# Dummy matmuls in two forced waits, a changed bias copy, and an output sum prepared ahead, in a fused transformer block

## The chip, the core and the metric

The kernel runs on one core of one Trainium2 chip. The core has a matrix engine (TensorE, PE in the profile, with its weight loads shown as PEld), a vector engine (VectorE, DVE), an engine for activation functions (ScalarE, ACT), a general one (GpSimd, POOL) and a sync engine (SP) that issues the DMAs here. Each engine runs its own list of instructions in order and waits on semaphores for the others. Matmuls write to PSUM, which has 8 banks of 512 float32 columns on 128 partitions. The metric is the device time of one execution, in microseconds.

## The reference

The input x is [1, 2048, 1024] in bf16; there are 32 heads of width 32, and the hidden width of the second half is 3584.

```python
h  = x + A(layernorm(x))
h2 = h + B(layernorm(h))

def A(x):                                   # attention, no mask
    q, k, v = split(x @ wqkv)               # 32 heads of 32
    p = softmax(q @ k.T * 32 ** -0.5)
    return (p @ v) @ wo

def B(x):                                   # feed-forward
    return gelu(x @ w1 + b1, tanh form) @ w2 + b2
```

## The kernel before

**A planner writes the order.** The Python code does not call the engines directly. `plan.task` appends an instruction to the list of its engine, works out which semaphores it must wait for, and adds its estimated `cost` to a clock for that engine (`plan.free`). `plan.ready` says when the inputs and the bank of a possible next step should be there. A loop (from line 1751) picks TensorE's next step by these planned times. The order is therefore fixed when the kernel is built, and a changed cost can change it.

**Stages.** First, all 2048 rows are normalized and transposed, and the first keys, queries and values are made (to about 52 us). Then comes the attention stage: 512 units, each for one group of 4 heads, 256 queries and 256 keys. One unit is a burst of 8 matmuls for scores (`qk`, line 1121, recorded at L1130) into 4 banks, then two exponentials on ScalarE over two banks each (L1139). The score banks are 0 to 5, as three pairs that rotate, so a burst can be issued as soon as the exponential that read the pair before has ended. The products with V and the row sums (`pv`, L1215) go to bank 6. For some units VectorE first adds the two halves of the exponentials (`fold`, L1164), which saves TensorE one of four steps. "Quad" below means four matmuls side by side on 32 output partitions each.

**Filling.** Between the bursts TensorE does "fill" work: first the remaining keys, queries and values, later the output projection and the whole feed-forward part (`ffn`, line 1463) of the query block before. Fill has only bank 7, so each result must be copied out by VectorE before the next fill starts. There are four query blocks of 512 rows; the fourth block's feed-forward part is the tail, after the last exponential (`tail`, line 1643).

**Forced waits.** Before a new group of heads starts in the first query block, its largest key norm must be known, because the exponential's bias is made from it. `until(mark, lax)` (line 1050) then runs pending `pv` steps and fill until the mark is there: a key projection, its copy to KT and its square on VectorE (lines 582, 583), the sums of squares (`sumsq`, line 628), a diagonal matrix (`spread`, line 643), a matmul with the ones matrix, a maximum (line 646) and the bias (`bias_of`, line 672).

**Feed-forward.** For each of 28 slices of 128 hidden columns, `evac` (line 1537) copies the bank to `gT`, adds b1 and halves (L1538). Per two slices a chain of four operations makes the gelu (L1550 to L1553; L1552 is a tanh on ScalarE). With y = x/2 the halved copy is used on both sides of the formula, so no factor is left at the end. `rows_out` (line 1429) multiplies by w2, adds b2 from the bank (L1448), adds the residual `hch` (L1451), and stores. `early_slices` makes 6 pairs of slices of the fourth block ahead of the tail (L1638).

**Tail.** Its gelu is one ScalarE instruction (L1678), and its output goes through `rows_out` as well: 8 calls, each for two row tiles and 256 output columns, with 56 matmuls into one bank. `load_b2` comes after the last weights in SP's list.

Of the kernel before, what the change touches and what calls it, by code (L numbers as in the profile page):

```python
# [235 lines left out]
def build_kernel(nc, A_x, A_wqkv, A_wo, B_w1, B_b1, B_w2, B_b2, out):  # L236
# [9 lines left out]
    SCALE = DH ** -0.5  # L246
    SAFE = 70.0
    EPS_BF = 1.0013580322265625e-05
    GC = 8.0 * 0.044715
    GB = 2.0 / GC  # L250
    GK = GC * math.sqrt(2.0 / math.pi)
    QF = 3.0
    KEEP = 7
# [796 lines left out]
    def until(mark, lax=False):  # L1050
        while mark not in marks:
            service(plan.free[E.PE])
            t = plan.free[E.PE]
            if lax and pending and fill_ready() > t + 60:
                e = sums[0] if sums and (due_sum() or plan.ready(E.PE, pv_reads(sums[0]), []) <= t + 150) else pending[0]
                if all(m_ in marks for m_ in v_marks(e)) and plan.ready(E.PE, pv_reads(e), [B_ps[OD]] if starts(e) else []) <= t + 150:
                    pv()
                    continue
            if not do_fill():
                raise RuntimeError(f"never made: {mark}")  # L1060

    biased = set()
    pending = deque()
# [365 lines left out]
    def rows_out(ci, q, t, w2_, gT, B_g, g_ch, ost, B_ost, hch, B_hch, b2s, coming=None):  # L1429
# [6 lines left out]
        for lo_fc, hi_fc, u in ((0, cut, 0), (0, cut, 1), (cut, FC, 0), (cut, FC, 1)):  # L1436
            lo = (t + u) * P
            for fc in range(lo_fc, hi_fc):
                if fc % 8 == 0 and coming:
                    coming.popleft()()  # L1440
                if fc % 2 == 0:
                    yield Need(B_g(fc) + B_g(fc + 1) + [B_w2_[fc // 2]], [B_ps[bank]] if u == 0 and fc == 0 else [],
                               [g_ch[fc + 1]] if fc + 1 in g_ch else [])
                wide(bank, u * 256, 256, gT[:, fc, lo:lo + P], w2[:, fc, :], fc == 0, fc == FC - 1,
                     B_g(fc) + [B_w2_[fc // 2]], [B_ps[bank]] if fc in (0, FC - 1) else [], fc == FC - 1, quad)
        o = (q * 2 + t // 2) % len(B_ost)
        b2_, B_b2_ = b2s
        dve(lambda v: v.tensor_tensor(ost[:, o, :, :], ps[:, bank, :].rearrange("p (u c) -> p u c", u=2),  # L1448
                                      b2_[:, q * 256:(q + 1) * 256].unsqueeze(1).to_broadcast([P, 2, 256]), ALU.add),
            reads=[B_ps[bank]] + B_b2_, writes=[B_ost[o]], cost=690)  # L1450
        add = (E.DVE, lambda v: v.tensor_tensor(ost[:, o, :, :], ost[:, o, :, :], hch[:, t:t + 2, q * 256:(q + 1) * 256], ALU.add),  # L1451
               [B_ost[o]] + [B_hch[2 * (t + u) + q // 2] for u in range(2)], [B_ost[o]], 430)
        r0 = CH[ci][0] + t * P

        def store():
            dma(out2[r0:r0 + 2 * P, q * 256:(q + 1) * 256].rearrange("(u p) c -> p u c", p=P), ost[:, o, :, :], 131072,
                reads=[B_ost[o]], lanes=lanes_o, is_out=True)
            if ci < NCH - 2 and q % 2:
                for u in range(2):
                    load_rows(r0 + 512 + u * P, t + u, q // 2)  # L1460
        stores.append(chain([add, ("call", store, [B_ost[o]], [], 0)]))

    def ffn(ci):
# [62 lines left out]
        for bk in range(FC // 2):  # L1526
            s = w1s[bk]
            for u in range(2):
                fc = bk * 2 + u
                if u == 1:  # L1530
                    load_w1(bk + len(B_w1_) - 1)
                if fc == FC // 2:
                    w2s = [load_w2(ci, 0, f["w2_off"])]
                if fc >= FC // 2:
                    w2s[0][2].popleft()()

                def evac(bank, fc=fc):
# [74 lines left out]
    def early_slices():  # L1612
        if early["stop"]:
            return
        tail_gelus()
        gT, B_gT = early["gT"]
        w1, B_w1_ = early["w1"]
        hn, B_hn = last["hn", 0]
        coming = early["coming"]
        while early["n"] < FC // 2 - AHEAD and not early["stop"]:  # L1620
            bk = early["n"]
            early["n"] += 1
            if bk:
# [12 lines left out]
            for u in range(2):  # L1636
                fc = 2 * bk + u
                dve(lambda v, fc=fc, u=u: v.tensor_scalar(gT[:, fc, 0:256], ps[:, bank, u * 256:u * 256 + 256], b1f[:, fc:fc + 1], None, ALU.add),  # L1638
                    reads=[B_ps[bank], Bf_b1f], writes=[B_gT[2 * fc]], cost=420)
        while coming:  # L1640
            coming.popleft()()

    def tail():
# [83 lines left out]
            load_more()  # L1727
        while rest:
            rest.popleft()()
        b2s = load_b2(LAST, v_off + 28672)  # L1730
        ost, B_ost = sb("ost_t", [P, 8, 2, 256], dt.bfloat16, nbufs(8), at=f["x3_off"])
        hch, B_hch = last["hch"]
        for q in range(4):
            for t in (0, 2):
                yield from rows_out(LAST, q, t, w2s[q], gT, lambda fc: [B_gT[2 * fc + t // 2]], {}, ost, B_ost, hch, B_hch, b2s)
            if q < 2:
                w2s.append(load_w2(LAST, q + 2, v_off + q * 14336, True))

# [12 lines left out]
    while u < NU or pending:  # L1751
# [199 lines left out]
```

## Time and profile before

| what | value |
|---|---|
| runs shown | 1149.47, 1150.96, 1151.28 us; median 1150.96 us |
| profiled execution, its own time | 1149.56 us |
| its span, first to last instruction | 1147.8 us |
| PE busy / ACT busy / DVE busy | 1086.5 / 1042.0 / 683.3 us |
| mean granted TensorE clock | 0.996 |
| exponentials L1139 | 1024 instructions, 952.0 us busy, mean 1145 ns of one |
| copies L1538 | 84 instructions, 63.0 us busy, mean 750 ns |

The times of instructions on one engine overlap (an exponential takes 1145 ns, but the next starts before it has ended), so busy time is not count times mean. "Idle before" is the time in which the engine stood still ahead of the instruction, with the instruction that ended it. The granted clock (PEclk) is 1.00 at full speed and 0.50 at half.

### The profile page before, as it was taken

What the parts mean: (1) busy time and instruction counts of PE and PEld (TensorE: products, weight loads), DVE (VectorE), ACT (ScalarE), POOL (GpSimd) and SP (SyncE); (2) the same over time, 40 slices, a digit from 0 to 9 for tenths busy, and PEclk for the clock granted to TensorE, in tenths of its full rate; (3) what the DMA queues carried; (4) which work ended last, traced back from release to release, by engine and by line L of the source; (5) the groups of instructions that cost most, each with busy time, mean ns of one, the idle gap of its engine ahead of it and who ended that gap; (6) DMA issues with size and microseconds to landing.
All of it is one profiled execution on the core that took longest, in us unless ns stands there. A gap on an engine that the chain in (4) does not pass through costs nothing.

```text
span 1147.8 us, 54608 instructions
## 1 busy us (share of the span) xinstructions
PE 1086.5 (95%) x25370; PEld 658.6 (57%) x25370; DVE 683.3 (60%) x1219; ACT 1042.0 (91%) x1158; POOL 21.2 (2%) x59
## 2 busy tenths in 40 slices
PE   6999999899998999999999999999999999999998
PEld 3646456464444445767444446675544476676887
DVE  8564565555666778545567787545678755556011
ACT  7798999899999999999999999999999999996410
POOL 2100000000000000000000000000000000000000
PEclk9999999999999999999999999999999999999999
DMA  9201000003341244342613343321223332426923
GB/s 264 58 21 40 15 9 3 21 4 103 67 85 58 76 117 115 92 122 60 135 30 95 90 126 99 96 82 31 77 77 109 107 110 72 83 81 187 246 79 87
DMA packets 197941, 98.43 MB, mean 86 GB/s; under 512 B 53328, under 2 KB 194640, under 8 KB 197712
## 3 DMA queue, kind: packets, MB, share of 16 engines
q1 hardware_dynamic: 197712, 94.93, 30.9%
q8 instruction: 198, 3.24, 1.2%
q14 instruction: 31, 0.25, 0.1%
HBM read 88.09 MB, written 4.19 MB: 80 GB/s over the span
## 4 chain that ended last, share of the span: by engine, by line
ACT 50%; PE 33%; issue 10%; DVE 6%; DMA 0%; POOL 0%; ACTq 0%; DVEq 0%; POOLq 0%
ACT PT L1139 47%; PE ps L529 13%; PE ps L524 8%; PE ps L1215 5%; PE ps L1130 4%; ACT tm L1552 3%; DVE lnst L481 1%; PE ps L803 1%; DVE Rg L1228 1%; DVE Rg L1226 1%; DVE QT L1230 1%; PE ps L858 1%; DVE rcp L1227 0%; DVE gT L1538 0%; DVE gT L1553 0%
## 5 line engine op out<-in xcount | busy, mean ns | idle before, releaser
L1139 ACT ACTIVATE PT<-ps 128x1024 bf16<-128x1024 f32 x1024 | 952.0, 1145 | 13.4 <-DVE biasm L681 9.7
L1164 DVE TENSOR_TENSOR FS<-PT 128x1024 bf16<-128x1024 bf16 x252 | 172.2, 688 | 146.7 <-ACT PT L1139 119.0
L1215 PE MATMUL ps<-PT,V 128*32 128x256 bf16 x4096 | 224.9, 274 | 11.6 <-ACT PT L1139 6.1
L1130 PE MATMUL ps<-QT,KT 32*128 32x256 bf16 x4096 | 203.9, 273 | 18.1 <-ACT PT L1139 14.5
L529 PE MATMUL ps<-hnT,w 128*32 128x512 bf16 x2688 | 172.6, 381 | 6.1 <-DVE gT L1538 4.5
L529 PE MATMUL ps<-w,gT 128*32 128x256 bf16 x5376 | 172.6, 273 | 0.7 <-issue 0.6
L1130 PEld LDWEIGHTS ps<-QT,KT 32*128 32x128 bf16 x4096 | 61.1, 92 | 168.0 <-ACT PT L1139 157.7
L529 PEld LDWEIGHTS ps<-w,gT 128*32 128x32 bf16 x5376 | 141.1, 97 | 10.5 <-issue 5.6
L1215 PEld LDWEIGHTS ps<-PT,V 128*32 128x32 bf16 x4096 | 106.0, 96 | 62.0 <-ACT PT L1139 16.2
L1215 PE MATMUL ps<-PT,ones 128*32 128x256 bf16 x2080 | 132.3, 274 | 0.0
L529 PEld LDWEIGHTS ps<-hnT,w 128*32 128x32 bf16 x2688 | 61.5, 96 | 75.5 <-issue 28.4
L1538 DVE TENSOR_SCALAR gT<-ps,b1f 128x512 bf16<-128x512 f32 x84 | 63.0, 750 | 46.0 <-PE ps L529 44.4
L1215 PE MATMUL ps<-FS,ones 128*32 128x256 bf16 x1008 | 72.4, 277 | 0.0
L1215 PEld LDWEIGHTS ps<-PT,ones 128*32 128x32 bf16 x2080 | 56.4, 97 | 10.1
L529 PE MATMUL ps<-xnTe,wk 128*32 128x512 bf16 x832 | 56.6, 395 | 4.3 <-DVE kmax L646 2.3
L1553 DVE SCALAR_TENSOR_TENSOR gT<-tm,gT 128x1024 bf16<-128x1024 bf16 x42 | 51.1, 1219 | 1.4 <-ACT tm L1552 1.0
L1551 DVE SCALAR_TENSOR_TENSOR tm<-tm,gT 128x1024 bf16<-128x1024 bf16 x42 | 51.3, 1222 | 0.9
L1552 ACT ACTIVATE tm<-tm 128x1024 bf16<-128x1024 bf16 x42 | 50.1, 1193 | 0.0
L524 PE MATMUL ps<-w,gT_t 128*128 128x256 bf16 x448 | 49.1, 273 | 0.0
L1448 DVE TENSOR_TENSOR ost_t<-ps,b 128x512 bf16<-128x512 f32 x8 | 5.5, 692 | 72.6 <-PE ps L524 72.6
L524 PEld LDWEIGHTS ps<-w,gT_t 128*128 128x128 bf16 x448 | 43.8, 98 | 5.1
L1678 ACT ACTIVATE gT_t<-ps,b1f 128x256 bf16<-128x256 f32 (+1 forms) x36 | 17.2, 518 | 28.5 <-PE ps L524 28.5
(140 smaller groups left out, 931.4 us busy)
## 6 DMA issues: line engine op xcount, KB each, us to landing
w<-in_B_w_dram SPq DMA_DIRECT2D x42, 512.0 KB, 3.8
w<-in_B_w_dram SPq DMA_DIRECT2D x168, 128.0 KB, 3.6
w_t<-in_B_w_dram SPq DMA_DIRECT2D x12, 512.0 KB, 6.7
xr<-in_A_x_dram SPq DMA_DIRECT2D x16, 256.0 KB, 6.9
wk<-in_A_wqkv_dram SPq DMA_DIRECT2D x16, 256.0 KB, 3.2
wq<-in_A_wqkv_dram SPq DMA_DIRECT2D x16, 256.0 KB, 4.7
w_e<-in_B_w_dram SPq DMA_DIRECT2D x32, 128.0 KB, 2.4
w<-in_B_w_dram SPq DMA_DIRECT2D x14, 256.0 KB, 5.5
```

The costliest lines, as they stand in the source:

```text
L481: steps.append((E.DVE, lambda v, c=c: v.bn_stats(lnst[:, s, i, c * 6:(c + 1) * 6], x_ap[:, c * 512:(c + 1) * 512]), [B_x], [B], 690))
L524: pe(lambda p: p.matmul(ps[:, bank, lo:lo + n], lhsT, rhs, start=start, stop=stop), reads=reads, writes=writes, inc=inc, cost=mm(n))
L529: pe(lambda p, r=r: p.matmul(ps[32 * r:32 * r + 32, bank, lo:lo + n], lhsT[:, 32 * r:32 * r + 32], rhs, start=start, stop=stop, tile_posit ...
L1130: pe(lambda p, k=k, kt=kt, r=r, b=b: p.matmul(ps[:, b, k * 256:(k + 1) * 256], KT[32 * r:32 * r + 32, g, kt * P:(kt + 1) * P], QT[32 * r:3 ...
L1139: act(lambda a, safe, i=i, b=b: a.activation(PT[:, o_, 2 * i:2 * i + 2, :], ps[:, b:b + 2, :], ACT.Exp, bias=0.0 if safe else biasm[:, g, ...
L1164: dve(lambda v: v.tensor_tensor(FS[:, f_, :, :], PT[:, o_, :, 0:256], PT[:, o_, :, 256:512], ALU.add), reads=B_PT[o_], writes=[B_FS[f_]], ...
L1215: pe(lambda p, d=d, r=r, lhsT=lhsT, rhs=rhs, n=n: p.matmul(ps[32 * r:32 * r + 32, OD, d * 256:(d + 1) * 256], lhsT, rhs, start=(start and ...
L1538: dve(lambda v: v.tensor_scalar(gT[:, fc, 0:w], ps[:, bank, 0:w], b1f[:, fc:fc + 1], 0.5, ALU.add, ALU.mult), reads=[B_ps[bank], Bf_b1f], ...
L1551: (E.DVE, lambda v: v.scalar_tensor_tensor(t_, t_, GB, x_, ALU.add, ALU.mult), [Bt] + Bx, [Bt], 1220),
L1552: (E.Activation, lambda a: a.activation(t_, t_, ACT.Tanh, scale=GK), [Bt], [Bt], 946),
L1553: (E.DVE, lambda v: v.scalar_tensor_tensor(x_, t_, 1.0, x_, ALU.add, ALU.mult), [Bt] + Bx, Bx, 1220)])
L1678: act(lambda a: a.activation(gT[:, fc, lo:lo + n], ps[:, bank, o:o + n], ACT.Gelu_apprx_tanh, bias=b1f[:, fc:fc + 1], scale=1.0), reads=[B ...
```

## The change

There are three parts.

1. A new function `awake(t)` is called with the planned time of TensorE's next useful step, in `until` where that is a forced wait, and in the main loop where ScalarE has nothing left by the plan. As long as more than 330 ns of planned waiting are left, it adds one quad that multiplies the ones matrix by itself (512 columns) into the first bank of the next score burst. That burst starts a new sum there, so nothing of it is kept.
2. The copy with b1 becomes a two-tensor addition, whose second operand is b1's column repeated over the slice, without the halving (84 copies in `ffn`, 12 in `early_slices`). The constants of the gelu change to match, and the factor 0.5 moves into the b2 addition of `rows_out`, which becomes a three-operand instruction. The planned cost of a copy goes from 714 to 690.
3. In the tail, residual and b2 are summed ahead into `hb` (4 additions on VectorE, float32, at `xl_off`, in memory that held output-projection weights whose use has ended). Each output bank is then read once, by one addition, instead of two additions, and stored at once, in the list's order. The last of the 8 output steps is split into its two row tiles, each with a bank, an addition of 256 columns and a store of 64 KB of its own.

```diff
-    GC = 8.0 * 0.044715
-    GB = 2.0 / GC
+    GC = 0.044715
+    GB = 1.0 / GC
...
+            if lax:
+                awake(fill_ready())
             if not do_fill():
                 raise RuntimeError(f"never made: {mark}")
+
+    def awake(t):
+        b = qk_banks(u)[0]
+        while t < INF and max(plan.free[E.PE], plan.ready(E.PE, [], [B_ps[b]])) + 330 < t:
+            for r in range(4):
+                pe(lambda p, r=r: p.matmul(ps[32 * r:32 * r + 32, b, :], ones_pp[:, 0:32], ones_pp[:].unsqueeze(1).to_broadcast([P, 4, P]),
+                                           start=True, stop=True, tile_position=(0, 32 * r), skip_group_check=True),
+                   reads=[B_ones], writes=[B_ps[b]] if r in (0, 3) else [], inc=r == 3, cost=mm(512) if r == 0 else 1, kind="C")
...
+        if ci == LAST:
+            hb, B_hb = b2s
+            if lone is not None:
+                r0, t, o = r0 + lone * P, t + lone, (o + lone) % len(B_ost)
+                dve(lambda v: v.tensor_tensor(ost[:, o, lone, :], ps[:, bank, lone * 256:lone * 256 + 256], hb[:, t, q * 256:(q + 1) * 256], ALU.add),
+                    reads=[B_ps[bank], B_hb[t]], writes=[B_ost[o]], cost=430)
+                dma(out2[r0:r0 + P, q * 256:(q + 1) * 256], ost[:, o, lone, :], 65536, reads=[B_ost[o]], lanes=lanes_o, is_out=True)
+                return
...
-        dve(lambda v: v.tensor_tensor(ost[:, o, :, :], ps[:, bank, :].rearrange("p (u c) -> p u c", u=2),
-                                      b2_[:, q * 256:(q + 1) * 256].unsqueeze(1).to_broadcast([P, 2, 256]), ALU.add),
+        dve(lambda v: v.scalar_tensor_tensor(ost[:, o, :, :], ps[:, bank, :].rearrange("p (u c) -> p u c", u=2), 0.5 if ci < LAST else 1.0,
+                                             b2_[:, q * 256:(q + 1) * 256].unsqueeze(1).to_broadcast([P, 2, 256]), ALU.mult, ALU.add),
...
-                    dve(lambda v: v.tensor_scalar(gT[:, fc, 0:w], ps[:, bank, 0:w], b1f[:, fc:fc + 1], 0.5, ALU.add, ALU.mult),
-                        reads=[B_ps[bank], Bf_b1f], writes=[B_gT[fc]], cost=100 + 1.2 * w)
+                    dve(lambda v: v.tensor_tensor(gT[:, fc, 0:w], ps[:, bank, 0:w], b1f[:, fc:fc + 1].to_broadcast([P, w]), ALU.add),
+                        reads=[B_ps[bank], Bf_b1f], writes=[B_gT[fc]], cost=690)
...
+        hb, B_hb = b2s = sb("hb", [P, 4, D], dt.float32, nbufs(4), at=xl_off)
+        for t4 in range(4):
+            dve(lambda v, t4=t4: v.tensor_tensor(hb[:, t4, :], hch[:, t4, :], b2_[:], ALU.add),
+                reads=B_hch[2 * t4:2 * t4 + 2] + B_b2_, writes=[B_hb[t4]], cost=1220)
         for q in range(4):
-            for t in (0, 2):
+            for t, lone in (((0, None), (2, None)) if q < 3 else ((0, None), (2, 0), (2, 1))):
...
             best = min(q_r, p_r if p_r + TURN + step <= due else INF, f_r if f_r + TURN + step <= due else INF)
+            if plan.free[E.Activation] <= t:
+                awake(best)
```

More of the change, by code (lines that the diff above doesn't have):

```diff
@@ L1427, in load_b2, with rows_out @@
         return b2_, B
-    def rows_out(ci, q, t, w2_, gT, B_g, g_ch, ost, B_ost, hch, B_hch, b2s, coming=None):
+    def rows_out(ci, q, t, w2_, gT, B_g, g_ch, ost, B_ost, hch, B_hch, b2s, coming=None, lone=None):
         w2, B_w2_, parts = w2_
@@ L1436, in rows_out @@
         for lo_fc, hi_fc, u in ((0, cut, 0), (0, cut, 1), (cut, FC, 0), (cut, FC, 1)):
+            if lone is not None and u != lone:
+                continue
             lo = (t + u) * P
@@ L1441, in rows_out @@
                 if fc % 2 == 0:
-                    yield Need(B_g(fc) + B_g(fc + 1) + [B_w2_[fc // 2]], [B_ps[bank]] if u == 0 and fc == 0 else [],
+                    yield Need(B_g(fc) + B_g(fc + 1) + [B_w2_[fc // 2]], [B_ps[bank]] if u == (lone or 0) and fc == 0 else [],
                                [g_ch[fc + 1]] if fc + 1 in g_ch else [])
@@ L1446, in rows_out @@
         o = (q * 2 + t // 2) % len(B_ost)
+        r0 = CH[ci][0] + t * P
+        if ci == LAST:
[6 more added lines that the diff above has]
+                return
+            dve(lambda v: v.tensor_tensor(ost[:, o, :, :], ps[:, bank, :].rearrange("p (u c) -> p u c", u=2), hb[:, t:t + 2, q * 256:(q + 1) * 256], ALU.add),
+                reads=[B_ps[bank]] + B_hb[t:t + 2], writes=[B_ost[o]], cost=690)
+            dma(out2[r0:r0 + 2 * P, q * 256:(q + 1) * 256].rearrange("(u p) c -> p u c", p=P), ost[:, o, :, :], 131072,
+                reads=[B_ost[o]], lanes=lanes_o, is_out=True)
+            return
         b2_, B_b2_ = b2s
-        dve(lambda v: v.tensor_tensor(ost[:, o, :, :], ps[:, bank, :].rearrange("p (u c) -> p u c", u=2),
-                                      b2_[:, q * 256:(q + 1) * 256].unsqueeze(1).to_broadcast([P, 2, 256]), ALU.add),
+        dve(lambda v: v.scalar_tensor_tensor(ost[:, o, :, :], ps[:, bank, :].rearrange("p (u c) -> p u c", u=2), 0.5 if ci < LAST else 1.0,
+                                             b2_[:, q * 256:(q + 1) * 256].unsqueeze(1).to_broadcast([P, 2, 256]), ALU.mult, ALU.add),
             reads=[B_ps[bank]] + B_b2_, writes=[B_ost[o]], cost=690)
@@ L1452, in rows_out @@
                [B_ost[o]] + [B_hch[2 * (t + u) + q // 2] for u in range(2)], [B_ost[o]], 430)
-        r0 = CH[ci][0] + t * P
         def store():
@@ L1637, in early_slices @@
                 fc = 2 * bk + u
-                dve(lambda v, fc=fc, u=u: v.tensor_scalar(gT[:, fc, 0:256], ps[:, bank, u * 256:u * 256 + 256], b1f[:, fc:fc + 1], None, ALU.add),
+                dve(lambda v, fc=fc, u=u: v.tensor_tensor(gT[:, fc, 0:256], ps[:, bank, u * 256:u * 256 + 256], b1f[:, fc:fc + 1].to_broadcast([P, 256]), ALU.add),
                     reads=[B_ps[bank], Bf_b1f], writes=[B_gT[2 * fc]], cost=420)
@@ L1729, in tail @@
             rest.popleft()()
-        b2s = load_b2(LAST, v_off + 28672)
+        b2_, B_b2_ = load_b2(LAST, v_off + 28672)
         ost, B_ost = sb("ost_t", [P, 8, 2, 256], dt.bfloat16, nbufs(8), at=f["x3_off"])
         hch, B_hch = last["hch"]
+        hb, B_hb = b2s = sb("hb", [P, 4, D], dt.float32, nbufs(4), at=xl_off)
+        for t4 in range(4):
+            dve(lambda v, t4=t4: v.tensor_tensor(hb[:, t4, :], hch[:, t4, :], b2_[:], ALU.add),
+                reads=B_hch[2 * t4:2 * t4 + 2] + B_b2_, writes=[B_hb[t4]], cost=1220)
         for q in range(4):
-            for t in (0, 2):
-                yield from rows_out(LAST, q, t, w2s[q], gT, lambda fc: [B_gT[2 * fc + t // 2]], {}, ost, B_ost, hch, B_hch, b2s)
+            for t, lone in (((0, None), (2, None)) if q < 3 else ((0, None), (2, 0), (2, 1))):
+                yield from rows_out(LAST, q, t, w2s[q], gT, lambda fc: [B_gT[2 * fc + t // 2]], {}, ost, B_ost, hch, B_hch, b2s, lone=lone)
             if q < 2:
```

## The prediction

> **What bounds the kernel now.** I read the page first (busy times and groups), then busy time by stretch, then the timeline where ScalarE stands still, then the timeline of the end.
>
> ```profile
> PE 1086.5 (95%) x25370; PEld 658.6 (57%) x25370; DVE 683.3 (60%) x1219; ACT 1042.0 (91%) x1158; POOL 21.2 (2%) x59
> ...
> L1139 ACT ACTIVATE PT<-ps 128x1024 bf16<-128x1024 f32 x1024 | 952.0, 1145 | 13.4 <-DVE biasm L681 9.7
> ```
>
> ScalarE's 91% hides two stages. From 52 us (first exponential) to 1046 us it almost never stops: 13.4 us of idle in front of 1024 exponentials, 9.7 of them in two waits for the bias. From there to the end TensorE is the bound. So the change can gain in three places only: those 13.4 us, the tail's matmuls, and what follows the last matmul. VectorE is at 60%, and shorter work on it gains nothing unless ScalarE waits for it.
>
> The two waits for the bias, from the timeline; each line has start, length, engine and operation, count, and idle before:
>
> ```profile
> 116.19 1.94 ACT L1139 ACTIVATE PT<-ps 128x1024 bf16<-128x1024 f32 x2 [4.84 <-DVE biasm L681]
> ...
> 119.34 1.94 ACT L1139 ACTIVATE PT<-ps 128x1024 bf16<-128x1024 f32 x2 [1.21 <-PE ps L1130]
> ...
> 210.80 1.94 ACT L1139 ACTIVATE PT<-ps 128x1024 bf16<-128x1024 f32 x2 [4.81 <-DVE biasm L681]
> ...
> 213.21 4.79 ACT L1139 ACTIVATE PT<-ps 128x1024 bf16<-128x1024 f32 x5 [0.48 <-PE ps L1130]
> ```
>
> After each wait comes a second, shorter gap, and it waits for TensorE's scores. The stretches say why (length, then busy PE, PEld, DVE, ACT, POOL; granted clock; DMA):
>
> ```profile
> 112.01:115.42 3.41, 1.27 (x36) 0.62 (x32) 2.99 (x9) 0.00 (x0) 0.00 (x0) 1.00 0.02 8
> 115.42:118.83 3.41, 3.41 (x32) 1.06 (x32) 0.54 (x4) 1.94 (x2) 0.00 (x0) 0.50 0.02 5
> 207.58:210.99 3.41, 1.70 (x36) 0.78 (x36) 2.84 (x11) 0.19 (x1) 0.00 (x0) 1.00 0.00 0
> 210.99:214.40 3.41, 3.41 (x48) 1.04 (x36) 1.12 (x2) 2.93 (x4) 0.00 (x0) 0.50 0.01 2
> 344.11:347.53 3.42, 2.03 (x56) 0.91 (x45) 3.15 (x7) 3.42 (x4) 0.00 (x0) 1.00 0.00 0
> 821.98:825.39 3.41, 1.78 (x48) 0.70 (x43) 1.91 (x6) 3.41 (x5) 1.14 (x3) 1.00 0.91 274
> 825.39:828.80 3.41, 3.41 (x100) 2.50 (x96) 1.38 (x3) 2.85 (x4) 0.00 (x0) 0.50 0.42 121
> ```
>
> The clock drops three times, to 0.50 for 3.41 us each. The starts, 115.42, 210.99 and 825.39, lie 28 and 180 times 3.413 us apart, so the gate works on a fixed grid. Cutting the execution along that grid, the only stretches with under 1.8 us of busy PE after the start are the three before the drops (1.27, 1.70, 1.78); the next, 2.03, keeps the full clock. So it goes by the busy time of a stretch (between 52% and 59%), not by one long gap: the longest gaps here are 0.98 and 1.16 us. At half clock 32 fill matmuls take 3.60 us (at 115.36) against 1.91 (at 110.30); the score burst stands behind them.
>
> **The dummies.** Nine quads are added, in four places: one ahead of the projection that ran at 110.30, four ahead of the ones-matmul at 113.63; two and two at the second wait (204.90 and 208.23). Eight such quads of 512 columns took 1.91 us, so one is 0.24. Wait 1: 1.27 + 4 x 0.24 = 2.2 us busy in the poor stretch; wait 2: 1.70 + 2 x 0.24 = 2.2. Both are above 2.03, so the clock should hold. The banks they write were last read by exponentials that have ended by then, as the ScalarE stands still.
>
> What goes: ScalarE's loss at 119.34. With 7 exponentials in 6.57 us, they end 0.904 apart; the one at 119.34 ended (1.94 - 0.90) after its start, at 120.38, and the one before at 118.13: 2.25, so 1.3 us lost. The same sum at 213.21 gives 0.7. What is late next: at full clock the fill ends at 115.36 + 1.91 = 117.3, and the burst's bank is free when the first exponential after the wait ends (about 117.2). Scores of 0.4 us plus a hop come by about 117.9, before 118.13. So both gaps go whole: -2.0.
>
> What they cost: queued behind the first quad are the projection, its copy to KT, the square, the diagonal matrix and thus the bias. TensorE stood idle for only 0.11 us there (pv ended at 110.19), so the quad delays this chain by 0.24 - 0.11 = 0.13 us. Bounds: 0 to 0.24. The four quads (112.65 + 0.96 = 113.61) end as the ones-matmul becomes ready (113.63); were they late, its reader, the maximum at 115.03, still leaves 1.1 us of cover, because VectorE first does a head's division (L1226 to L1230). At wait 2, 0.48 us lies in gaps of 0.89 and 0.55: nothing. Sum: -2.0 + 0.13 = -1.85.
>
> [...] Measured on the busy times of this trace, I moved the grid through 69 positions: 35 have a stretch under 1.78 us at wait 1, 26 at wait 2. So another execution may have had neither drop, and the part is worth between 0 and -2.0. I take -1.85, since the profiled execution had both, and keep 0 for the range.
>
> **The copy with b1.** 84 copies of 750 ns become two-tensor additions; L1448 (687), L1336 (690) and, for a float32 second operand, L1230 (424 at 256 columns, as against 476 for the 12 early ones) say 690 and 424: 84 x 60 + 12 x 52 = 5.7 us less on VectorE. In `rows_out` 24 additions of 687 become three-operand ones; L1551 has 1222 for 1024 columns, so about 690; if PSUM costs it as it did the old copy, 750: 1.4 us more. All of it lies beside exponentials. ScalarE's idle outside the two waits and their gaps is 13.4 - 9.7 - 1.7 = 2.0 us, 0.56 of it the third drop, so the gain is 0 to 2.0. I take 0: a freed 60 ns lets fill start earlier, not scores.
>
> **The new order.** From about 300 us on the planner lays fill, pv and scores anew, since a copy now costs 690 instead of 714. Counting matmuls between score bursts in both lists, bursts with over 1.8 us of work ahead of them are 52 before and 53 after, with over 2.5 us 13 and 10; folds fall from 252 to 250, two quads more. The plan was 36 ns too low for a copy and is now right. I take 0, between -1.4 (all small stalls go) and +1.5 (they double). Cover: TensorE waits for ScalarE ahead of 460 of 512 bursts, 157.7 us in all, 0.34 each; one quad of fill (0.24) in front fits.
>
> **The tail.** The lists are equal from the end of the last feed-forward part on; PE's last matmul stays where it is.
>
> ```profile
> 1144.31 0.69 DVE L1448 TENSOR_TENSOR ost_t<-ps,b 128x512 bf16<-128x512 f32 x1 [4.96 <-PE ps L524]
> 1145.04 0.42 DVE L1451 TENSOR_TENSOR ost_t<-ost_t,hch_t 128x512 bf16<-128x512 bf16 x1
> 1145.49 0.37 SPq L290 DMA_DIRECT2D out_dram<-ost_t  x1
> ```
>
> After it, 0.69 + 0.03 + 0.42 become one addition of 256 columns, 0.42: the store starts 0.73 us sooner. Its own time (2.28 us, issue to span's end) is for 128 KB; 64 KB should take up to 0.25 less. I take -0.85. The other stores end earlier on the same lanes. `hb`: 4 x 1.22 = 4.9 us, after b2 has landed (issued at 1082.86, 4.3 us: about 1088), done by 1093; the first output bank is ready at 1101.5, 8 us of cover. On SP's queue the weights of quarters 2 and 3 now stand behind one more store: issue at about 1108.4 instead of 1107.62, landed 6.3 us later at 1115 to 1116, needed at 1119.8. Hidden by 4 us; without that cover up to 1.1 us each.
>
> **Sum.** -1.85 + 0 + 0 - 0.85 = -2.7. Against the profiled execution's 1149.56 that is 1146.9; it lies 1.4 under the median of the runs, so for a median I give 1150.96 - 2.7 = 1148.3.
>
> **Rivals.** (1) The dummies gain nothing, because the drop doesn't come from the filled gaps or the median run has no drop. For it: the grid's luck, and runs that spread by 1.8 us though nothing changed. Against it: the clean border between 1.78 and 2.03. Left are the tail and the 0.13: 1150.96 - 0.7 = 1150.3, no measurable change. [...]
> (2) Slower: the new order lets scores come late in the feed-forward stretches. It needs about 5 us of new stalls to pass +0.2%, 2.3 + 2.7; such stalls cost 2.0 us in all before, the largest 0.56. For it: 460 of 512 bursts have only 0.34 us of cover. Against it: equal burst counts. At three times the stalls plus the third drop's repeats (0.7 each): about 1153.5.
> (3) The new order also takes away the third drop and the small stalls: -1.4 more, 1146.9.
>
> **How the numbers follow.** A measurement of this kernel can tell about 0.2% (2.3 us) from no change. The forecast gets 0.55, rival 1 0.24, rival 2 0.11, rival 3 0.10. Of the forecast a tenth (0.05) falls within 0.2%, since 1148.3 lies just under the border of 1148.66. Faster 0.50 + 0.10 = 0.60; same 0.24 + 0.05 = 0.29; slower 0.11. The range runs from rival 3 with 1.1 less for the profiled execution's place under the median (1145.8) to rival 1 with 0.9 for its delay and the runs' spread (1151.2); rival 2 and as much again below are left out.
>
> **What would show it.** Right: the clock at 1.00 through 116 to 119 and 211 to 215, no gap after the two waits, first-wait idle 4.8 to 5.1, L1538's successor at 690 ns, one addition of 0.42 us and a 64 KB store at the end. Wrong: a drop in spite of 2.2 us of busy PE; idle in front of exponentials above 12 us; the ones-matmul later than 113.9; an output addition that waits for `hb`.

## The result, and the profile after

| what | before | after |
|---|---|---|
| median of the compared runs (7 and 7) | 1150.93 us | 1147.21 us |
| lowest and highest | 1149.47, 1152.45 | 1146.53, 1147.39 |
| profiled execution, its own time | 1149.56 us | 1147.39 us |
| its span | 1147.8 us | 1145.6 us |
| mean granted clock, profiled execution | 0.996 | 1.000 |

The ratio is 0.9968 with a 95% interval of 0.9956 to 0.9979: 3.7 us faster (2.4 to 5.1). The runs also lie closer together, within 0.9 us where those of before spread over 3.0.

The page of the changed kernel (engine busy times; then two groups: count, busy time, mean ns of one, idle time ahead of them):

```profile
span 1145.6 us, 54689 instructions
PE 1086.6 (95%) x25409; PEld 657.3 (57%) x25414; DVE 678.0 (59%) x1214; ACT 1041.8 (91%) x1158; POOL 21.2 (2%) x59
...
L1149 ACT ACTIVATE PT<-ps 128x1024 bf16<-128x1024 f32 x1024 | 954.1, 1164 | 11.7 <-DVE biasm L681 9.7
...
L1563 DVE TENSOR_TENSOR gT<-ps,b1f 128x512 bf16<-128x512 f32 x84 | 58.0, 690 | 49.2 <-PE ps L529 48.5
```

ScalarE's idle time ahead of the exponentials falls from 13.4 to 11.7 us, and the 9.7 us of the two waits for the bias stay. The copies take the 690 ns that were expected, and VectorE is busy 5.3 us less (678.0 against 683.3), with no wait of ScalarE that shows a use for it.

The timeline of the changed kernel at the first wait and at the second (start, length, engine and operation, count, idle before):

```profile
109.88 0.40 PE L632 MATMUL ps<-sqk,blk 128*32 128x512 bf16 x4
110.88 0.39 PE L1068 MATMUL ps<-ones_pp 128*32 128x512 bf16 x4
111.17 1.91 PE L529 MATMUL ps<-xnTe,wk 128*32 128x512 bf16 x32
113.33 1.05 PE L1068 MATMUL ps<-ones_pp 128*32 128x512 bf16 x16
116.23 1.91 PE L529 MATMUL ps<-xnTe,wk 128*32 128x512 bf16 x32 [1.16 <-DVE kmax L646]
...
117.06 4.69 ACT L1149 ACTIVATE PT<-ps 128x1024 bf16<-128x1024 f32 x5 [4.84 <-DVE biasm L681]
...
210.35 7.44 ACT L1149 ACTIVATE PT<-ps 128x1024 bf16<-128x1024 f32 x8 [4.81 <-DVE biasm L681]
```

L1068 is the dummies: one quad, then four. After the idle 4.84 us ScalarE runs without a gap to the end of the view (five exponentials; eight at the second wait), where before it stopped after two. The fill projection at 116.23 takes 1.91 us; before, its counterpart took 3.60 at half clock. The idle gap of 1.16 us ahead of it is still there, and the clock holds in spite of it. By stretches (length, then busy time of PE, PEld, DVE, ACT, POOL; granted clock; DMA):

```profile
113.00:116.41 3.41, 2.13 (x52) 1.04 (x47) 3.07 (x10) 0.00 (x0) 0.00 (x0) 1.00 0.05 16
116.41:119.82 3.41, 2.90 (x60) 1.21 (x52) 1.58 (x5) 2.76 (x4) 0.00 (x0) 1.00 0.00 0
206.50:209.91 3.41, 2.13 (x56) 1.13 (x52) 3.17 (x11) 0.00 (x0) 0.00 (x0) 1.00 0.00 0
209.91:213.32 3.41, 2.90 (x60) 1.09 (x48) 1.40 (x4) 2.96 (x4) 0.00 (x0) 1.00 0.03 7
```

The two poor stretches, 1.27 and 1.70 us of busy PE before, have 2.13 each, and the stretch behind each has the full clock. These stretches do not lie on one grid (206.50 is not a whole number of 3.413 us behind 113.00): this trace shows no change of the clock by which its grid could be laid. They are the poorest places. A stretch of 3.41 us moved in steps of 0.05 us has at least 2.13 us of busy PE at the first wait and 2.14 at the second, wherever it starts; before, it goes down to 1.27 and 1.70.

The end, from the timeline of the changed kernel:

```profile
1136.97 0.69 DVE L1468 TENSOR_TENSOR ost_t<-ps,hb 128x512 bf16<-128x512 f32 x1 [5.42 <-PE ps L524]
...
1140.03 0.42 DVE L1464 TENSOR_TENSOR ost_t<-ps,hb 128x256 bf16<-128x256 f32 x1 [2.36 <-PE ps L524]
1143.09 0.42 DVE L1464 TENSOR_TENSOR ost_t<-ps,hb 128x256 bf16<-128x256 f32 x1 [2.63 <-PE ps L524]
```

One addition of 0.42 us stands behind the last matmul, and the span ends 2.55 us after that matmul (3.50 before).

**Where the profiled executions differ.** The span is 2.2 us shorter. Cut at the first exponential, the last one, and the last matmul:

| part | before | after | difference |
|---|---|---|---|
| start to first exponential | 52.26 | 53.12 | +0.87 |
| first to last exponential | 994.04 | 991.95 | -2.09 |
| last exponential to last matmul | 97.97 | 97.98 | +0.01 |
| last matmul to end of span | 3.50 | 2.55 | -0.95 |

The +0.87 is not the change: no instruction is moved there. The two traces part at the first value projections, with two lines of before:

```profile
11.51 2.63 PE L858 MATMUL ps<-wv,xnTe 128*128 128x256 bf16 x16
...
52.26 1.94 ACT L1139 ACTIVATE PT<-ps 128x1024 bf16<-128x1024 f32 x2 [0.36 <-issue]
```

and two of after:

```profile
11.58 3.51 PE L858 MATMUL ps<-wv,xnTe 128*128 128x256 bf16 x16
...
53.12 1.02 ACT L1149 ACTIVATE PT<-ps 128x1024 bf16<-128x1024 f32 x1 [0.36 <-issue]
```

The same 16 matmuls took 0.88 us longer, because they came to full speed later: most took 417 ns each up to 13.02 us before and up to about 14.8 after, those behind it in the trace of before 273. The two profiles differ by 2.2 us and the medians by 3.7; this handicap is 0.87 of the 1.5 us between them. The rest isn't accounted for: the profiled execution of before, at 1149.56 us, lies 1.4 under its median.

The -2.09 of the attention stage is made of the two gaps after the waits (-2.0, as in the prediction), the third drop, which is gone too (-0.8), and about +0.7 that the rest of the stage takes longer. Of that, 0.5 is idle time ahead of exponentials: 11.7 us, against 13.39 - 1.21 - 0.48 - 0.56 = 11.1 before without the gaps of the three drops. Two of the new small gaps in the timeline of the changed kernel:

```profile
926.83 3.80 ACT L1149 ACTIVATE PT<-ps 128x1024 bf16<-128x1024 f32 x4 [0.30 <-PE ps L1140]
930.92 9.52 ACT L1149 ACTIVATE PT<-ps 128x1024 bf16<-128x1024 f32 x10 [0.30 <-PE ps L1140]
```

The +0.7 is a balance. When the ends of the 1024 exponentials are compared one by one in the two traces, the changed kernel gains a further 1.0 us by 470 us and loses 0.3 from there to 820 and 1.4 between 880 and 945. Of the 1.0, 0.66 lies at one place, where TensorE of before stands still for 0.61 us though the profile shows nothing that it waits for:

```profile
459.45 1.38 PE L529 MATMUL ps<-w,gT 128*32 128x256 bf16 x42 [0.61 <-issue]
```

The scores behind it come late, and ScalarE is idle for 0.56 us (at 461.21). The changed kernel has no such gap there. It has one at 703.92, of 0.47 us, behind another standstill of this kind (0.56 us at 701.94).

### The profile page after: what moved, and what is told of

It reads as the page before. It is cut to its first block, busy times and chain, and to the rows that moved or that the text cites. A ratio compares the mean times of both kernels' runs of the same rounds, so it can differ in the third digit from the quotient of the medians.

```text
span 1145.6 us, 54689 instructions
## 1 busy us (share of the span) xinstructions
PE 1086.6 (95%) x25409; PEld 657.3 (57%) x25414; DVE 678.0 (59%) x1214; ACT 1041.8 (91%) x1158; POOL 21.2 (2%) x59
## 4 chain that ended last, share of the span: by engine, by line
ACT 49%; PE 33%; issue 11%; DVE 5%; DMA 0%; POOL 0%; ACTq 0%; DVEq 0%; SPq 0%; POOLq 0%
ACT PT L1149 46%; PE ps L529 13%; PE ps L524 8%; PE ps L1225 6%; PE ps L1140 4%; ACT tm L1577 2%; DVE lnst L481 1%; PE ps L803 1%; DVE Rg L1236 1%; DVE Rg L1238 1%; PE ps L858 1%; DVE QT L1240 1%; DVE gT L1578 0%; PE ps L511 0%; DVE rcp L1237 0%
## 5 line engine op out<-in xcount | busy, mean ns | idle before, releaser
L1149 ACT ACTIVATE PT<-ps 128x1024 bf16<-128x1024 f32 x1024 | 954.1, 1164 | 11.7 <-DVE biasm L681 9.7
L1563 DVE TENSOR_TENSOR gT<-ps,b1f 128x512 bf16<-128x512 f32 x84 | 58.0, 690 | 49.2 <-PE ps L529 48.5
L529 PE MATMUL ps<-xnTe,wk 128*32 128x512 bf16 x832 | 54.2, 381 | 3.4 <-DVE kmax L646 2.3
L1577 ACT ACTIVATE tm<-tm 128x1024 bf16<-128x1024 bf16 x42 | 52.5, 1250 | 0.0
L582 DVE CAST KT<-ps 128x512 bf16<-128x512 f32 x28 | 19.4, 692 | 35.9 <-PE ps L529 35.6
```

Of the source, the lines that this page charges most:

```text
L529: pe(lambda p, r=r: p.matmul(ps[32 * r:32 * r + 32, bank, lo:lo + n], lhsT[:, 32 * r:32 * r + 32], rhs, start=start, stop=stop, tile_posit ...
L582: dve(lambda v: v.tensor_copy(k_ap, ps[:, bank, :]), reads=[B_ps[bank]], writes=[B_KT[g][tc]], cost=690)
L1149: act(lambda a, safe, i=i, b=b: a.activation(PT[:, o_, 2 * i:2 * i + 2, :], ps[:, b:b + 2, :], ACT.Exp, bias=0.0 if safe else biasm[:, g, ...
L1563: dve(lambda v: v.tensor_tensor(gT[:, fc, 0:w], ps[:, bank, 0:w], b1f[:, fc:fc + 1].to_broadcast([P, w]), ALU.add), reads=[B_ps[bank], Bf_ ...
```

## The experiments

Theory A is the prediction's: the clock drops after a stretch of the grid with too little busy PE, the dummies lift that busy time, and the rest of the gain is the shorter end. Against it stand the prediction's rivals (the dummies gain nothing, or the new order decides), and two that came up with the result. C: any activity on TensorE keeps the clock up, however short. D: the forced waits exist because the first query block (block 1) has too little other work, so that a wait removed in one place comes back in another. Ratios are to the kernel before on the same chip. The first four experiments share 35 runs of before (median 1149.84 us); those with 32 columns, with all key norms earlier and with the last step whole share 23 (1150.26); the one with two key norms earlier has 13 (1150.16).

### The dummies alone

Part 1 was put into the kernel before; everything else on TensorE keeps its order.

```diff
+            if lax:
+                awake(fill_ready())
             if not do_fill():
...
+            if plan.free[E.Activation] <= t:
+                awake(best)
```

> The kernel before with the dummy matmuls alone; the order of all other instructions is that of before. Theory A (dummies hold the clock at the two forced waits): granted clock 1.000 or 0.999 in every run where the kernel before has 0.996 to 0.998, no idle in front of the second exponential pair after each wait, 1.1 to 2.7 us faster (ratio 0.9977 to 0.9990). Theory B (the median run of before has no drop, or the drop has another cause): ratio 0.9995 to 1.0005, clock as before. By the trace of after, the first quad should cost nothing: the forced wait stays 4.84 us.

Measured: median 1147.61 us of 11 runs, ratio 0.9978 (0.9970 to 0.9987), or -2.5 us (-1.5 to -3.4). Its timeline at the two waits:

```profile
117.07 4.69 ACT L1149 ACTIVATE PT<-ps 128x1024 bf16<-128x1024 f32 x5 [4.84 <-DVE biasm L681]
...
210.36 6.52 ACT L1149 ACTIVATE PT<-ps 128x1024 bf16<-128x1024 f32 x7 [4.82 <-DVE biasm L681]
```

Both second gaps are gone with nothing else changed in the kernel. Only the third drop is left, as its stretches show:

```profile
820.10:823.48 3.38, 1.75 (x44) 0.69 (x40) 1.88 (x6) 3.38 (x5) 1.14 (x3) 1.00 1.09 324
823.48:826.90 3.42, 3.42 (x96) 2.43 (x92) 1.31 (x4) 2.77 (x4) 0.00 (x0) 0.50 0.23 59
```

Ten of the 11 runs have a clock of 1.000 or 0.999, as expected, and one has 0.998; of the 35 runs of before, 15 have 0.999 or 1.000. In this trace the stretches of 3.41 us from 113.00 and from 206.50 have 2.13 us of busy PE each, and no drop follows either wait. So the dummies gain by themselves, by the two medians about two thirds of the whole. Not all of it is the drops': between the first and the last exponential this trace is 2.7 us shorter than that of before, -2.0 at the two waits and -0.66 at 461 us, where it lacks the gap of 0.56.

### The tail alone

Part 3 was put into the kernel before.

```diff
+        hb, B_hb = b2s = sb("hb", [P, 4, D], dt.float32, nbufs(4), at=xl_off)
...
-            for t in (0, 2):
-                yield from rows_out(LAST, q, t, ...)
+            for t, lone in (((0, None), (2, None)) if q < 3 else ((0, None), (2, 0), (2, 1))):
+                yield from rows_out(LAST, q, t, ..., lone=lone)
```

> The kernel before with the tail's part alone; matmuls in the order of before. Both theories: only the stretch after the last matmul changes, from 3.50 us (before) to about 2.55 (after), so 0.95 us faster, ratio 0.9992; clock as in the kernel before. If the 4 sums ahead collided with something, the first output addition would come later than 1101.5 us.

Measured: median 1149.09 us of 11 runs, ratio 0.9990 (0.9980 to 0.9999), or -1.2 us (-0.1 to -2.3). In the profile the span ends 2.56 us after the last matmul, against 3.50: 0.94 us, where the forecast had 0.85. The runs alone could not tell this from much less, because the clock drops of before are still in them. Up to the last matmul this profiled execution had three, one of them where before had none (same columns as above):

```profile
147.37:150.78 3.41, 1.96 (x48) 0.85 (x44) 3.27 (x10) 3.41 (x5) 0.00 (x0) 1.00 0.00 0
150.78:154.19 3.41, 3.41 (x47) 1.30 (x40) 0.67 (x2) 2.13 (x3) 0.00 (x0) 0.50 0.02 5
```

TensorE's order is the same here as before, and the stretch ahead of the drop has 1.96 us of busy PE. The drop cost a gap of 1.28 us ahead of the exponential at 153.84. This speaks against a part of the prediction, the border "between 1.78 and 2.03"; more on that below.

### The copy alone

Part 2 was put into the kernel before, with the order that its new planned cost brings.

```diff
-    dve(lambda v: v.tensor_scalar(gT[:, fc, 0:w], ps[:, bank, 0:w], b1f[:, fc:fc + 1], 0.5, ALU.add, ALU.mult),
-        ..., cost=100 + 1.2 * w)
+    dve(lambda v: v.tensor_tensor(gT[:, fc, 0:w], ps[:, bank, 0:w], b1f[:, fc:fc + 1].to_broadcast([P, w]), ALU.add),
+        ..., cost=690)
```

> The kernel before with the b1 copy (and the gelu constants and the three-operand b2 addition) alone, so with the new order of the feed-forward stretches. Theory A: 84 copies at 690 instead of 750 ns, no gain in time by themselves: ratio 0.999 to 1.001, the two drops at the forced waits stay. Theory B: what is missing from the dummies comes from here, ratio 0.997 to 0.9985, with small stalls of the exponentials gone. The third drop, at about 826 us, may go or stay.

Measured: median 1148.56 us of 12 runs, ratio 0.9992 (0.9981 to 1.0002). That is -0.9 us with an interval from -2.2 to +0.2, so a small gain is possible and not shown. The profiled execution had one drop (at 116.25). Its idle time ahead of exponentials is 12.5 us, and 12.5 - 1.08 = 11.4 without that drop's gap; before has 13.39 - 1.21 - 0.48 - 0.56 = 11.1 without its three. So ScalarE waits as long as ever, and the 5.0 us that VectorE saves on the copies (58.0 us busy against 63.0) show no effect at the end. The third drop is gone, and the new order is enough for that: in the changed kernel, which has this order too, a stretch of 3.41 us near 822 has at least 2.30 us of busy PE, wherever it starts; in the kernel before it goes down to 1.78.

### The change without the dummies

```diff
-            if lax:
-                awake(fill_ready())
...
-            if plan.free[E.Activation] <= t:
-                awake(best)
```

> The changed kernel without the dummy matmuls, its other instructions in the changed order. Theory A: the drops come back in the runs (clock 0.997 to 0.999), and it lies 1.1 to 2.7 us above the changed kernel's 1147.2: ratio to before 0.998 to 0.9993. Theory B: it is as fast as the changed kernel, ratio 0.9968.

Measured: median 1148.47 us of 11 runs, ratio 0.9980 (0.9971 to 0.9989). The gap after the second wait is back in its timeline:

```profile
210.77 1.94 ACT L1139 ACTIVATE PT<-ps 128x1024 bf16<-128x1024 f32 x2 [4.81 <-DVE biasm L681]
...
213.88 2.85 ACT L1139 ACTIVATE PT<-ps 128x1024 bf16<-128x1024 f32 x3 [1.17 <-PE ps L1130]
```

A drop at 210.05 made it; the first wait had none in this execution. Nine of the 11 runs had a mean clock under 1.000, as A expected of all, against one of 7 in the changed kernel. By the two ratios the dummies are worth 0.9980 - 0.9968, or 1.4 us, on top of the other parts. These are runs of different chips, and the intervals overlap, so this is weaker than the first experiment. The two runs at 1.000 took 1145.98 and 1146.01 us, 2.2 less than the mean of the eight at 0.999 (1148.21): where luck spares a run the drop, it needs no dummies. The dummies have a price as well. Against the trace of the changed kernel this one loses 1.26 us at the drop and 0.9 near 461, where it has the gap of before again (0.66 us, at 461.49), but it gains 0.6 near 704 and 1.1 near 927, where it lacks the changed kernel's small gaps. So those gaps come with the dummies and not with the new order.

### Dummies of 32 columns

The changed kernel with as many dummies in the same places, each with 32 columns where it had 512. Only their length changes.

```diff
-    pe(lambda p, r=r: p.matmul(ps[32 * r:32 * r + 32, b, :], ones_pp[:, 0:32], ones_pp[:].unsqueeze(1).to_broadcast([P, 4, P]),
+    pe(lambda p, r=r: p.matmul(ps[32 * r:32 * r + 32, b, 0:32], ones_pp[:, 0:32], ones_pp[:, 0:32],
```

> The changed kernel, whose dummy matmuls have 32 columns instead of 512: same number, same places, almost no busy time. Theory A (the gate goes by the busy time of a stretch): the drops at about 117 and 211 us come back by the luck of the grid, clock 0.997 to 0.999 in most runs, and the time is that of the changed kernel without dummies, ratio to before 0.998. Rival C (any activity in the gap holds the clock, or the number of matmuls counts): clock 1.000 and ratio 0.997 as in the changed kernel.

Measured: median 1148.65 us of 10 runs, ratio 0.9984 (0.9973 to 0.9996); one run of 10 at a clock of 1.000, the others at 0.996 to 0.999. Its stretches at the second wait:

```profile
206.86:210.27 3.41, 1.74 (x60) 1.20 (x52) 3.10 (x10) 0.00 (x0) 0.00 (x0) 1.00 0.00 0
210.28:213.69 3.41, 3.41 (x40) 1.16 (x32) 0.57 (x4) 1.94 (x2) 0.00 (x0) 0.50 0.02 5
```

60 matmuls but only 1.74 us of busy PE, and the clock drops. The changed kernel has 56 in such a stretch, 2.13 us busy, and it holds. (The first of these stretches lies on the grid of its trace; the changed kernel's was laid by hand at the poorest place.) So rival C falls: it is the time that the dummies fill, not their number. In the changed kernel the ones matrix multiplied by itself, 512 columns and 379 ns a matmul, held the clock.

### All key norms earlier

If the largest key norm were known earlier, the waits of 4.8 us themselves might go. In the changed kernel the second step of every norm (diagonal matrix, ones-matmul, maximum) was put right behind the first, in place of one projection later.

```diff
-                    yield from mix(proj_k(g, tc), knorm_a(last))
-                elif tc == 1 and last is not None:
-                    yield from mix(proj_k(g, tc), knorm_b(last))
+                    yield from mix(proj_k(g, tc), mix(knorm_b(last), knorm_a(last)))
...
-            if g < 6:
-                yield from mix(proj_q(g, 0), (knorm_a, knorm_b)[g - 4](4))
+            if g == 4:
+                yield from mix(proj_q(g, 0), mix(knorm_b(4), knorm_a(4)))
```

> The changed kernel, with the second step of each key norm (diagonal, ones-matmul, maximum) put right behind the first, ahead of the next key projection. Theory A: the dummies only shorten what follows a forced wait; the wait itself (2 x 4.8 us) is a chain over VectorE that stands behind a projection of 1.9 us, so it should shrink to 1 to 3 us each: 3 to 7 us faster than the changed kernel, ratio to before 0.991 to 0.9945. Rival D: TensorE's fill is what block 1 really lacks, the wait only moves to the next group's keys: same time as the changed kernel, ratio 0.996 to 0.9975.

Measured: median 1150.94 us of 12 runs, ratio 1.0005 (0.9996 to 1.0014). The expectation of A here, 0.991 to 0.9945, fell, and so did that of D, 0.996 to 0.9975: this kernel is slower than the changed one. The timeline shows where the gain went:

```profile
112.79 7.44 ACT L1147 ACTIVATE PT<-ps 128x1024 bf16<-128x1024 f32 x8 [0.62 <-DVE biasm L681]
...
208.42 1.02 ACT L1147 ACTIVATE PT<-ps 128x1024 bf16<-128x1024 f32 x1 [6.93 <-DVE biasm L681]
...
303.56 2.86 ACT L1147 ACTIVATE PT<-ps 128x1024 bf16<-128x1024 f32 x3 [4.96 <-DVE biasm L696]
```

The first wait shrinks from 4.84 to 0.62 us, the second grows from 4.81 to 6.93, and a third of 4.96 appears: 12.5 us in place of 9.65. The wait moves, as D has it. (This execution also had a drop at 287.03, with a gap of 1.20 us.)

### Two key norms earlier

The same edit for two head groups alone, so that the third wait of the last experiment has no cause.

```diff
-                if tc == 0 and last is not None:
+                if tc == 0 and last is not None and last in (1, 2):
+                    yield from mix(proj_k(g, tc), mix(knorm_b(last), knorm_a(last)))
+                elif tc == 0 and last is not None:
                     yield from mix(proj_k(g, tc), knorm_a(last))
-                elif tc == 1 and last is not None:
+                elif tc == 1 and last is not None and not (last in (1, 2)):
```

> The changed kernel with the second step of the key norm put forward for two head groups only (the wait at 117 us has one of them; the wait at 210 us keeps its old order). Rival D (fill is what block 1 lacks, a shorter chain only moves the wait): the first wait falls from 4.84 to about 0.7 us, the second grows from 4.81 to 8 or 9, ratio to before 0.9965 to 0.998, no better than the changed kernel. Theory A (the chain's length is the loss): second wait unchanged, ratio 0.993.

Measured: median 1148.14 us of 10 runs, ratio 0.9984 (0.9974 to 0.9993).

```profile
112.26 13.86 ACT L1151 ACTIVATE PT<-ps 128x1024 bf16<-128x1024 f32 x15 [0.61 <-DVE biasm L681]
...
210.97 14.82 ACT L1151 ACTIVATE PT<-ps 128x1024 bf16<-128x1024 f32 x16 [10.05 <-DVE biasm L681]
```

The first wait is gone but for 0.61 us, and the second has taken over more than all of it: 10.66 us together, against 9.65 in the changed kernel. The direction is D's; the second wait and the ratio lie a little above its figures (8 or 9 us, 0.998). That the fill runs out is D's reason for it and was not tested by itself: no run gave the first query block more fill. No version here beats the changed kernel.

### The last step whole

The changed kernel with its last output step not split into two row tiles, in one execution (1148.47 us), of which only the end is read.

```diff
-            for t, lone in (((0, None), (2, None)) if q < 3 else ((0, None), (2, 0), (2, 1))):
+            for t, lone in ((0, None), (2, None)):
```

> The changed kernel without the split of the last output step (one addition of 512 columns, one store of 128 KB). Of the 0.95 us gained behind the last matmul, leaving out the second addition should account for 0.45 (0.42 and a hop), the narrower addition for 0.27, the smaller store for the rest: here 3.05 us from the last matmul's end to the span's end.

```profile
1143.68 0.69 DVE L1468 TENSOR_TENSOR ost_t<-ps,hb 128x512 bf16<-128x512 f32 x1 [5.42 <-PE ps L524]
1144.39 0.37 SPq L290 DMA_DIRECT2D out_dram<-ost_t  x1
```

The span ends 3.03 us after the last matmul. Of the 0.95 us at the end, 3.50 - 3.03 = 0.47 come from the sum made ahead (an addition of 0.42, the 0.03 ahead of it, and 0.02 more) and 3.03 - 2.55 = 0.48 from the split: 0.69 - 0.42 = 0.27 for the shorter addition, and the 0.21 that are left go to the store of 64 KB in place of 128.

## Why the prediction was right

It said 1148.3 us, faster, and the changed kernel takes 1147.21, within its range; the forecast of -2.7 us lies inside the measured -2.4 to -5.1. Step by step:

**The dummies: right in mechanism, and near in size partly by luck.** Forecast -1.85 us; -2.5 (-1.5 to -3.4) alone. "So both gaps go whole" held: no gap after either wait, and -2.0 us in the profiles. The busy time came to 2.13 where 2.2 was forecast. But "I take -1.85, since the profiled execution had both" gave a median run both drops. By the prediction's own count of positions a mean run saves 35/69 x 1.3 + 26/69 x 0.7 = 0.9 us (an estimate). The clocks say as much: the mean over the runs is 0.9979 before and 0.9991 with the dummies alone, about 0.8 drops of 0.0015 fewer. The runs gained more than that, and 0.66 us of the rest may be the gap at 461 us, which the prediction did not consider. It is there in the traces of all four kernels without dummies (0.56, 0.28, 0.66 and 0.66 us) and not in those of the dummies alone, the changed kernel and the 32 columns; with all key norms earlier one of 0.98 is near there. Why the dummies take it away stays open.

The cost of the first quad, "0.24 - 0.11 = 0.13", was not there: the projection behind it started 1.29 us after the sums of squares in both kernels (109.01 to 110.30 before, 109.88 to 111.17 after). It needs bank 7, which VectorE has to read out first: in both traces it starts 0.15 us after the end of that read (L635, at 110.15 and 111.02). So the waits stayed at 4.84 and 4.81, in the lower part of the forecast's 4.8 to 5.1. The prediction looked at TensorE's idle time in front of the projection (0.11 us) and not at the bank that it also needed.

**"The clean border between 1.78 and 2.03": too strong.** It rested on one execution, and the reading of that one left out its end: the stretch with the last matmul, 1142.83 to 1146.25, has 1.44 us of busy PE, and the clock is at 1.00 from there to the span's end. In the traces with drops, each cut along its own grid, those up to the last matmul followed stretches with 1.27, 1.70 and 1.78 us (before), 1.36, 1.96 and 1.70 (tail alone), 1.27 (copy alone), 1.71 (without dummies), 1.74 (32 columns) and 1.75 in 3.38 us (dummies alone, the third drop). In the trace of before all from 2.03 up kept it. So 1.96 lost the clock where 1.44 kept it. The busy time of the records is modelled for matmuls, and by these cases it doesn't decide alone. The dummies' 2.13 lies above all that lost the clock, so the conclusion stood. A remedy that ended at 1.9 would have stood between the prediction's rows and would not have been safe. One such place is left in the changed kernel: near 147 us a stretch can have as little as 1.96 us, the busy time after which the tail alone lost the clock.

**"So another execution may have had neither drop": right, and a part of the spread.** Runs of one and the same kernel before, by their mean granted clock (one drop of 3.41 us at half speed is 0.0015 of 1148 us):

| mean clock | runs | mean time, us |
|---|---|---|
| 1.000 | 4 | 1147.91 |
| 0.999 | 21 | 1149.31 |
| 0.998 | 11 | 1149.88 |
| 0.997 | 18 | 1150.47 |
| 0.994 to 0.996 | 17 | 1150.83 |

These are the 71 runs of before beside the experiments. From the first row to the last the mean time rises by 2.9 us. Within the row of 0.999 single runs still go from 1147.52 to 1150.53, so the number of drops is only a part of what makes runs differ. The changed kernel has a clock of 1.000 in six of its 7 runs and 0.999 in one. So rival 1 ("the median run has no drop") was wrong: 4 runs of 71 had none. The prediction moved the grid with no trace at hand that shows it move; the traces together do: with the matmuls in the order of before, drops began at 115.42 and 210.99 us in the execution of before and at 116.64 and 212.22 in that of the tail alone, both pairs 28 times 3.413 us apart. The longest gap does not tell either: in the trace of before the clock fell at 825.39 with no gap above 0.52 us in the stretch ahead, and it stayed at 1.00 through and behind gaps of 1.17 us (at 346.95 and 361.84); in the changed kernel it was held with the gap of 1.16.

**The copy: zero was right within what could be measured.** -0.9 us (-2.2 to +0.2) alone, with 11.4 against 11.1 us of idle ahead of exponentials once the drops are taken off. The 690 ns were right.

**The new order: zero, but for the third drop.** It is gone: with the old order and the dummies 9 of 11 runs have a clock under 1.000, with the new order and the dummies 1 of 7. That is rival 3 in part (-0.8 us in the profiles). The small gaps of the changed kernel look like rival 2, but the new order without the dummies doesn't have them. Ahead of the one at 703.92 TensorE stood still without a wait that the profile shows (0.56 us, at 701.94), as before did at 459.45. What these standstills are, and why the dummies move them, was not followed further. The cover of 0.34 us that bursts have on the mean did not absorb them.

**The tail: right.** Forecast 0.73 and up to 0.25 more, taken as 0.85; measured 0.95, as 0.47 + 0.27 + 0.21. The 0.25 for the smaller store was the author's estimate, which no trace of before shows; in the changed kernel's the stores of 64 KB land 1.5 us after their issue in the median, those of 128 KB beside them 1.9. No output addition waits for `hb`.

**The sum.** The parts measured alone give -2.5 - 1.2 - 0.9 = -4.6, the whole -3.7, each with an interval of about a us either way. The medians moved by 1 us more than the forecast's -2.7, within the interval. The term that came out furthest is the dummies', 0.65 us larger alone than in the sum; the third drop, which no part was credited with and which goes with the new order, is of the same size. How much of the 1 us is either, and how much is chance, isn't settled.

## What to carry to other kernels

- Where the granted clock drops now and then, cut the trace along the grid of the drops (3.413 us here) and look at TensorE's busy time in the stretch before each one. If a stretch is poor because TensorE waits, matmuls whose result nobody keeps can fill it, provided that they are long enough to fill time (here 512 columns held the clock and 32 did not) and go into a bank that is idle anyway. Look then for new gaps elsewhere: here the added matmuls also moved standstills of TensorE at 461, 704 and 927 us.
- A kernel whose runs spread by 0.3% may be having a varying number of such drops (here 1147.91 us on the mean at a clock of 1.000, 1150.83 at 0.994 to 0.996); a single profile then shows one draw, and its times are no median.
- A forced wait that is shortened by doing its work earlier can come back as the next wait. Count the fill that is left for that one before moving it: here 4.2 us gained at one wait came back as 5.2 at the next.

## What the runs showed of the hardware that was not expected

**The start depends on the same luck.** When the matmuls of the start come to full speed differs from run to run, and the first exponential moves with it, though no instruction ahead of it differs:

| full speed at, us | first exponential at, us | kernel |
|---|---|---|
| 13.02 | 52.26 | before |
| 13.43 | 52.34 | two key norms earlier |
| 13.85 | 52.74 | copy alone |
| 13.96 | 52.85 | all key norms earlier |
| 14.25 | 52.75 | tail alone |
| 14.38 | 52.86 | last step whole |
| 14.52 | 53.14 | dummies alone |
| 15.49 | 53.55 | without dummies |
| 15.72 | 53.68 | 32 columns |

The rise to full speed lies on the same grid as the drops: from 13.02 to the first drop of before, at 115.42, are 30 whole stretches of 3.413 us, and from 15.49 to 210.05 without dummies 57. The table spans 1.4 us of the time of a run, as much as one of the smaller parts of the change, and no edit in the attention stage can reach it.

**A stretch of 1.96 us of busy PE lost the clock, one of 1.44 kept it.** The first is that from 147.37 us with the tail alone, the second that from 1142.83 before. So neither the longest gap nor the modelled busy time alone tells where the clock drops. What decides it stays open; no run here took it apart.
